# A fused Fourier filter, mixture layer and channel mixer on one core: forward units of batches 1 to 7 spread over more of the tiles

## The chip, the cores and the metric

The kernel runs on one core of a Trainium2 chip. The metric is the time of one execution on the device in microseconds. Before the change it is 3288.33 us, the median of three runs (3287.11 to 3288.41). The engines are named as in the profile: PE (matrix products), PEld (its weight loads), DVE (vector), ACT (scalar), POOL (GpSimd) and SP, which issues nearly all DMAs.

## The reference

Eight sequences of 3072 tokens with 256 channels go through three layers in float32:

```python
X = np.fft.rfft(x, axis=1)
y = np.fft.irfft(X * (filt_r + 1j * filt_i), n=S, axis=1)          # long filter, per channel
h = np.maximum(np.maximum(y @ w1, y @ w2), y @ w3)                 # 256 -> 768
x1 = h @ w_out                                                     # 768 -> 256
prev = x1 shifted by one token within its sequence
xk, xr = mu_k * x1 + (1 - mu_k) * prev, mu_r * x1 + (1 - mu_r) * prev
k = np.maximum(xk @ w_k, 0)                                        # 256 -> 1024
out = 1 / (1 + np.exp(-(xr @ w_r))) * ((k * k) @ w_v)
```

## The kernel before

Every product is made of three: both factors are split into a rounded high part (`xH`, cast by ACT) and the rest (`xL`, subtracted by POOL or DVE), and `mm3` (L121) multiplies high by high, high by low and low by high.

**Three stages.** First batch 0's filter and the weights of the middle layer, to about 150 us. Then the middle layer in 48 tiles of 512 tokens, six to a batch (`t` is the tile, `b` its batch, `g` its place in the batch), and beside tiles 0 to 41 the filter of batches 1 to 7. Last, from about 2060 us, the channel mixer in 48 tiles; the diff does not touch it.

**A tile of the middle layer** has six blocks `fblock` (18 products of 512 columns each; ACT copies the first result, DVE takes the maximum with the other two into `hm`, then `hH` on ACT and `hL` on POOL), then `stage_b` (the last step of the inverse transform of the next tile, products into `y`), then `x1_out` (36 products into `x`). For the next tile `untwiddle` makes `vp` on DVE from `vt`, which `load_v` fetches two tiles ahead from DRAM (`vs`), and ACT and POOL split it (`vH`, `vL`). An ordinary tile has 168 products.

**The filter of a batch** comes from the generator `fft_all` (L321). Its forward part has six units. For each one, `load_x` fetches `xt` (four DMAs, half of them from `xr`, a mirrored copy of x that `mirror_x` writes to DRAM by pairs of batches), `split_x` folds it on POOL (`xe`, two instructions) and splits it (`xH` on ACT, `xL` on POOL, two each), `dft_rows` puts six products into `re` and `im`, and `twiddle` turns these into `A` (per call two scalings `t` on ACT, two DVE instructions). Then for each half `h` of the channels DVE does a 12-point transform (`dft12`), a product with the filter `F`, a 12-point transform back, and the result `T` goes to `vs`. A small side path with four short products treats one frequency apart.

**What sets the order.** Instructions stand on each engine in the order in which the code issues them. `fft_all` yields a cost after each piece, or `STOP`. The `Meter` (L756) is called at 15 steps in a tile, two in each `fblock` and three in `x1_out`. At a step it goes on with the generator until the sum of the costs has reached the share that `share` asks for at this point, and it ends a step at a `STOP`. `done_at` says at which tile each batch's filter is to be done: 5, 11, 17 and so on. A batch costs `FFT_COST`: 6 units of `U_COST` = 2 and 88.6 for the rest, so 100.6, and in six tiles that is 16.8 a tile. `meter.need(b + 1)` at the last tile of a batch finishes that filter; `load_v` of the next tile follows at once there.

The forward units of a batch stand close together: each is `dft_rows`, the load for two units on, the whole split of the next unit, a `STOP`, both twiddles, and a `STOP`. Both halves of the mirroring for a pair are issued ahead of the loads of an odd batch's units.

Of the kernel before, what the change touches and what calls it, by code (L numbers as in the profile page):

```python
# [7 lines left out]
F32 = mybir.dt.float32  # L8
# [5 lines left out]
B, S, D = 8, 3072, 256  # L14
NF = 768
NF2 = 1024
P = 128
NH = D // P
# [74 lines left out]
def tile_fourier_moe_rwkv(ctx, tc, xl, fl, f0, dft24m, dft, idft, tw, w1, w2, w3, wo, muk, mur, wk, wv, wr, out):  # L93
# [162 lines left out]

    def mirror_x(p):
        for h in range(NH):  # L260
            rows = xl[p, h].rearrange("n g ab x -> g ab n x")[:, :, :63:-1]
            if p == 0:
                nc.sync.dma_start(out=xr[p][h].rearrange("(g ab) n x -> g ab n x", ab=2)[:, 1], in_=rows[:, 1])
            else:
                nc.sync.dma_start(out=xr[p][h], in_=rows.rearrange("g ab n x -> (g ab) n x"))

    def fetch_x(xt, b, u):
        lower = xl[b // 2, :, :, u, b % 2].rearrange("h n (o x) -> o n h x", o=2)
        upper = xr[b // 2][:, 2 * u + b % 2].rearrange("h n (o x) -> o n h x", o=2)
        for k in range(2):  # L270
            for odd in range(2):
                if k == 0:
                    rows = lower[odd, :64]
                elif b:
                    rows = upper[1 - odd]
                else:
                    rows = lower[odd, 64:]
                nc.sync.dma_start(out=xt[64 * odd:64 * odd + 64, k].rearrange("p (h x) -> p h x", h=NH), in_=rows)

    def fold(xe, xt, eng):  # L280
        tt(xe[:, 0], xt[:, 0], xt[:, 1], add, eng)
        tt(xe[:, 1], xt[:, 0], xt[:, 1], sub, eng)

    def dft_rows(xH, xL):
        re = bank([P, NH, 2, P], "re")
        im = bank([P, NH, 2, P], "im")
        for k, o in enumerate((re, im)):
            mm3(o.rearrange("p h q c -> p (h q c)"), dftH[:, k], dftL[:, k], xH[:, k], xL[:, k], True, True)
        return re, im
# [30 lines left out]

    def fft_all():  # L321
        xt_t, xs_t, ps_t, f_t = {}, {}, {}, {}

        def load_x(b, u):
            if b < B:
                xt_t[b, u] = fp.tile([P, 2, 512], F32, tag="xt", name="xt", bufs=2)
                fetch_x(xt_t[b, u], b, u)

        def split_x(b, u):
            xt = xt_t.pop((b, u))  # L330
            xe = fp.tile([P, 2, 512], F32, tag="xe", name="xe")
            fold(xe, xt, nc.gpsimd)
            xH = fp.tile([P, 2, 512], F32R, tag="xH", name="xH", bufs=2)
            xL = fp.tile([P, 2, 512], F32R, tag="xL", name="xL", bufs=2)
            for k in range(2):
                nc.scalar.copy(out=xH[:, k], in_=xe[:, k])
                tt(xL[:, k], xe[:, k], f32(xH[:, k]), sub, nc.gpsimd)
            xs_t[b, u] = (xH, xL)

        def twiddle(b, u, A, q):  # L340
            re, im = ps_t[b, u]
            s = 2 * u + q
            t1 = fp.tile([P, NH, P], F32, tag="t1", name="t1", bufs=2)
            t2 = fp.tile([P, NH, P], F32, tag="t2", name="t2", bufs=2)
            scaled(t1, im[:, :, q], nsinv(s))
            scaled(t2, re[:, :, q], sinv(s))
            for r, (a, t) in enumerate(((re, t1), (im, t2))):
                stt(A[:, :, s, r], a[:, :, q], cosv(s), t, mult, add)

        def load_f(h):  # L350
            f_t[h] = fp.tile([P, 2, M2, P], F32, tag="F", name="F")
            nc.sync.dma_start(out=f_t[h], in_=fl[h, :, :, :M2])

        mirror_x(0)
        load_f(0)
        load_x(1, 0)
        load_x(1, 1)
        yield STOP
        yield STOP
        yield STOP  # L360
        split_x(1, 0)
        yield STOP
        yield STOP
        for b in range(1, B):
            A = fp.tile([P, NH, M2, 2, P], F32, tag="A", name="A")
            if b % 2 and b + 1 < B:
                mirror_x((b + 1) // 2)
            for u in range(NU):
                ps_t[b, u] = dft_rows(*xs_t.pop((b, u)))
                if u + 2 < NU:  # L370
                    load_x(b, u + 2)
                if u + 1 < NU:
                    split_x(b, u + 1)
                yield STOP
                for q in range(2):
                    twiddle(b, u, A, q)
                    yield U_COST / 2
                ps_t.pop((b, u))
                yield STOP
            nc.sync.dma_start(out=rs[b].rearrange("(o h) s r c -> o (h s r c)", o=1), in_=A[0:1].rearrange("p h s r c -> p (h s r c)"))  # L380
            sidegen = side(b)
            for h in range(NH):
                X = A[:, h]
                T = fp.tile([P, M2, 2, P], F32, tag="T", name="T", bufs=2)
                F = f_t.pop(h)
                if h == NH - 1:
                    load_x(b + 1, 0)
                    load_x(b + 1, 1)
                fi = F[:, 1].rearrange("p (a s) c -> p a s c", s=4)[:, :, 2:4]
                nc.scalar.mul(out=fi, in_=fi, mul=-1.0)  # L390
                yield from dft12(X, T, 0)
                for g in range(3):
                    sl = slice(4 * g, 4 * g + 4)
                    for r in range(2):
                        tt(X[:, sl, r], T[:, sl, r], F[:, 0, sl], mult)
                    yield 1.3
                    for r in range(2):
                        tt(T[:, sl, r], T[:, sl, r], F[:, 1, sl], mult)
                    yield 1.3
                    tt(X[:, sl, 0], X[:, sl, 0], T[:, sl, 1], sub)  # L400
                    tt(X[:, sl, 1], X[:, sl, 1], T[:, sl, 0], add)
                    yield 1.3
                if b + 1 < B or h + 1 < NH:
                    load_f((h + 1) % NH)
                if h == NH - 1 and b + 1 < B:
                    split_x(b + 1, 0)
                for c in dft12(X, T, 1):
                    yield c
                    if h == NH - 1:
                        next(sidegen, None)  # L410
                nc.sync.dma_start(out=vs[b][:, h], in_=T)
                if h == NH - 1:
                    for _ in sidegen:
                        pass
                    done.add(b)
                yield 0.0
# [175 lines left out]
                    spread_f(c + 1, j)  # L592
            yield

    U_COST = 2.0
    FFT_COST = NU * U_COST + 2 * 44.3


# [284 lines left out]
    with tc.manual_schedule():  # L883
# [49 lines left out]
            pass  # L933


        meter, done_at = Meter(fft_all(), (B - 1) * FFT_COST), [0.0] + [6.0 * b - 1.0 for b in range(1, B)]

        def share(tau):
            for b in range(1, B):
# [5 lines left out]
        for t, (b, g) in enumerate(tiles):  # L945
            if t == len(tiles) - NTILE:
                meter.to(1.0)
                fctx.close()
                p2w = ctx.enter_context(tc.tile_pool(name="p2w", bufs=1, side="right"))
                tctx = ctx.enter_context(ExitStack())  # L950
                p2t = tctx.enter_context(tc.tile_pool(name="p2t", bufs=1, side="right"))
                meter = Meter(load_w2(p2w, p2t), 58.0)
                share = lambda tau, t0=float(t): (tau - t0) / (NTILE - 2)
            at[0] = float(t)

            def step(w):
                at[0] += w / TILE_STEPS
                meter.to(share(at[0]), CAP * w)

            last = t == len(tiles) - 1  # L960
            if last:
                meter.to(1.0)
                tctx.close()
                p2 = ctx.enter_context(tc.tile_pool(name="p2", bufs=1, side="right"))
                load_x1(0, p2)
                load_x1(1, p2)
            edge = g == NTILE - 1
            if edge and not last:
                meter.need(b + 1)
                load_v(t + 1)  # L970
            for f in range(FB1):
                fblock(t, f, step)
                if not last and f in ((2, 4) if edge else (1, 3)):
                    untwiddle(t + 1, f // 2 - 1 if edge else (f - 1) // 2)
                if f == 4 and t + 2 < len(tiles) and g != NTILE - 2:
                    load_v(t + 2)
                if last and f % 2:
                    shift_mix(0, f // 4, (f // 2) % 2, p2)
            y_t.pop(t)
            run_later()  # L980
            if not last:
                stage_b(t + 1)
            x1_out(t, step)
# [98 lines left out]
```

## Time and profile before

| | us |
|---|---|
| median of three runs (range) | 3288.33 (3287.11 to 3288.41) |
| the profiled execution | 3289.4 |
| its span, first to last instruction | 3287.6 |
| PE busy in the span | 3111.7 (95%) |
| DVE, ACT, POOL busy | 2159.7, 1481.7, 1335.0 |
| mean granted clock of PE | 0.978 |

The page gives for each engine the time in which some instruction of it ran. A row of 40 digits cuts the span into 40 slices of 82.2 us. The view by stretches answers the same for any stretch, so a stretch can be laid on a tile: from the first `fblock` product of a tile to the first one of the next. That view rounds to 0.1 us and counts an instruction at a border in both stretches. The waits view names what ended an engine's idle time before an instruction.

### The profile page before, as it was taken

The numbers are of one execution on the slowest core, as the hardware profiler recorded it, in microseconds if no ns is written. First come the engines' busy times: TensorE is split into PE (matmuls) and PEld (weight loads), VectorE is DVE, ScalarE is ACT, GpSimd is POOL, SyncE is SP. The second block draws the span as 40 slices with busy tenths as digits, with TensorE's granted clock in tenths as the row PEclk, the third lists the DMA queues.
The fourth block names the chain that finished last, engine by engine and source line by source line (L and its number), as shares of the span: only waits on it lengthen the run. The fifth ranks groups of instructions, "written<-read, shape, count | busy, mean of one in ns | idle before, by whom it ended". The sixth has DMA issues, their size and how long they took to land. (4 is left out here: it accounts for less than half of the span.)

```text
span 3287.6 us, 43694 instructions
## 1 busy us (share of the span) xinstructions
PE 3111.7 (95%) x16596; PEld 2644.5 (80%) x16596; DVE 2159.7 (66%) x2825; ACT 1481.7 (45%) x2744; POOL 1335.0 (41%) x988
## 2 busy tenths in 40 slices
PE   4689899799999899899999999999999999999999
PEld 2368688688788688788788888888999899989998
DVE  3769688588688588688587553555555565556555
ACT  3643333333433433433433443555555555555554
POOL 2263633533534523534533333344434443444433
PEclk7999999899999999999999999999999999999999
DMA  5622212312212312221211210111111111111110
GB/s 147 190 92 77 91 46 60 127 46 70 79 46 84 103 45 84 65 90 39 78 65 40 77 52 32 52 52 58 49 52 52 58 49 49 52 57 53 49 52 33
DMA packets 110743, 221.37 MB, mean 67 GB/s; under 512 B 11477, under 2 KB 51773, under 8 KB 108733
## 3 DMA queue, kind: packets, MB, share of 16 engines
q1 hardware_dynamic: 106244, 213.86, 20.1%
q10 hardware_dynamic: 4288, 4.72, 0.6%
q8 instruction: 130, 2.13, 0.3%
q14 instruction: 81, 0.66, 0.1%
HBM read 139.55 MB, written 90.00 MB: 70 GB/s over the span
## 5 line engine op out<-in xcount | busy, mean ns | idle before, releaser
L127 POOL TENSOR_TENSOR hL<-hm,hH 128x512 fp32r<-128x512 f32 x288 | 416.7, 1447 | 942.0 <-ACT hH L730 928.7
L127 DVE TENSOR_TENSOR hm<-p,hm 128x512 f32<-128x512 f32 x576 | 394.4, 686 | 325.9 <-PE p L124 260.6
L124 PE MATMUL pv<-wvh,kl 128*128 128x256 f32 x1536 | 433.0, 282 | 9.7 <-POOL kl L127 8.3
L127 POOL TENSOR_TENSOR ml<-tm,mh 128x512 fp32r<-128x512 f32 x192 | 248.6, 1295 | 456.3 <-ACT mh L819 456.3
L123 PE MATMUL pv<-wvl,kh 128*128 128x256 f32 x1536 | 428.1, 279 | 0.0
L122 PE MATMUL pv<-wvh,kh 128*128 128x256 f32 x1536 | 428.0, 279 | 0.0
L127 POOL TENSOR_TENSOR kl<-sq,kh 128x512 fp32r<-128x512 f32 x192 | 248.3, 1293 | 267.8 <-ACT kh L843 106.9
L722 ACT COPY hm<-p 128x512 f32<-128x512 f32 x288 | 168.6, 586 | 396.7 <-PE p L124 396.5
L819 ACT CAST mh<-tm 128x512 fp32r<-128x512 f32 x192 | 119.1, 620 | 495.4 <-DVE tm L130 495.4
L124 PEld LDWEIGHTS pv<-wvh,kl 128*128 128x128 f32 x1536 | 289.7, 189 | 19.5 <-POOL kl L127 19.5
L123 PE MATMUL pk<-ml,wkh 128*128 128x512 f32 x768 | 303.3, 395 | 0.1
L122 PE MATMUL pk<-mh,wkh 128*128 128x512 f32 x768 | 300.2, 391 | 0.0
L124 PE MATMUL pk<-mh,wkl 128*128 128x512 f32 x768 | 299.7, 390 | 0.0
L122 PEld LDWEIGHTS pv<-wvh,kh 128*128 128x128 f32 x1536 | 290.2, 189 | 0.0
L123 PEld LDWEIGHTS pv<-wvl,kh 128*128 128x128 f32 x1536 | 288.4, 188 | 0.0
L130 DVE SCALAR_TENSOR_TENSOR sq<-pk,rl 128x512 f32<-128x512 f32 x384 | 249.7, 680 | 58.2 <-ACT rl L838 58.2
L130 DVE SCALAR_TENSOR_TENSOR tm<-xt,mu_sb,tm 128x512 f32<-128x512 f32 x192 | 194.3, 1012 | 131.5 <-ACT tm L139 131.5
L730 ACT CAST hH<-hm 128x512 fp32r<-128x512 f32 x288 | 179.4, 623 | 189.6 <-DVE hm L127 189.0
L127 DVE TENSOR_TENSOR ot<-pv,sg 128x512 f32<-128x512 f32 x96 | 66.4, 692 | 301.4 <-issue 223.8
L127 DVE TENSOR_TENSOR kl<-sq,kh 128x512 fp32r<-128x512 f32 x192 | 221.3, 1152 | 31.7 <-ACT kh L843 15.6
L843 ACT ACTIVATE kh<-rl 128x512 fp32r<-128x512 f32 x384 | 240.8, 641 | 0.0
L122 PE MATMUL p<-yH,w1h 128*128 128x512 f32 x576 | 229.3, 398 | 2.6 <-DVE hm L127 1.9
(163 smaller groups left out, 8140.5 us busy)
## 6 DMA issues: line engine op xcount, KB each, us to landing
xt<-x1s SPq DMA_DIRECT2D x40, 768.0 KB
x1s<-xo SPq DMA_DIRECT2D x96, 256.0 KB
out_dram<-ot SPq DMA_DIRECT2D x96, 256.0 KB
F<-in_fl_dram SPq DMA_DIRECT2D x14, 1536.0 KB
vs<-T SPq DMA_DIRECT2D x14, 1536.0 KB
vt<-vs SPq DMA_DIRECT2D x42, 512.0 KB
xt<-in_xl_dram SPq DMA_DIRECT2D x108, 128.0 KB
xt<-xr SPq DMA_DIRECT2D x84, 128.0 KB
```

Of the source, the lines that this page charges most:

```text
L122: nc.tensor.matmul(o, lh, rh, start=first, stop=False)
L123: nc.tensor.matmul(o, lh, rl, start=False, stop=False)
L124: nc.tensor.matmul(o, ll, rh, start=False, stop=last)
L127: (eng or nc.vector).tensor_tensor(out=o, in0=a, in1=b, op=op)
L130: nc.vector.scalar_tensor_tensor(out=o, in0=a, scalar=s, in1=b, op0=op0, op1=op1)
L722: nc.scalar.copy(out=hm, in_=ps[0])
L730: nc.scalar.copy(out=hH, in_=hm)
L819: nc.scalar.copy(out=hi, in_=tf)
L843: nc.scalar.activation(out=kh, in_=rl, func=AF.Square)
```

## The change

The diff spreads the units. `split_x` becomes a generator of three pieces (fold; first half of the split; second half), and these stand between the two twiddles of the unit before. Units are counted through all batches, x is fetched two units ahead also across the end of a batch, and so the first unit of a batch is split before the transforms of the batch before it. `U_COST` goes from 2 to 6, so a batch costs 124.6. Each half of a mirroring stands apart: for batches 2 and 3 behind the loads in the first two units of batch 1, later ones ahead of the two halves of an even batch's transforms. From batch 2 on, `done_at` is 10.3, 16.3, 22.3 and so on; `meter.need` and the load of the next batch's first tile move into the last tile but one, behind its fifth `fblock`. Batch 1's filter still has to be done at tile 5, and its load stays there.

```diff
-        def split_x(b, u):
-            xt = xt_t.pop((b, u))
+        units = [(b, u) for b in range(1, B) for u in range(NU)]
...
+        def split_x(i):
+            if i == len(units):
+                return
+            xt = xt_t.pop(i)
             xe = fp.tile([P, 2, 512], F32, tag="xe", name="xe")
             fold(xe, xt, nc.gpsimd)
+            yield
...
             for k in range(2):
                 nc.scalar.copy(out=xH[:, k], in_=xe[:, k])
                 tt(xL[:, k], xe[:, k], f32(xH[:, k]), sub, nc.gpsimd)
+                if k == 0:
+                    yield
...
             for u in range(NU):
-                ps_t[b, u] = dft_rows(*xs_t.pop((b, u)))
-                if u + 2 < NU:
-                    load_x(b, u + 2)
-                if u + 1 < NU:
-                    split_x(b, u + 1)
+                i = NU * (b - 1) + u
+                ps_t[u] = dft_rows(*xs_t.pop(i))
+                load_x(i + 2)
+                if b == 1 and u < NH:
+                    mirror_x(1, u)
                 yield STOP
-                for q in range(2):
-                    twiddle(b, u, A, q)
-                    yield U_COST / 2
-                ps_t.pop((b, u))
-                yield STOP
+                sgen = split_x(i + 1)
+                twiddle(b, u, A, 0)
+                yield U_COST / 6
+                next(sgen, None)
+                yield U_COST / 4
+                twiddle(b, u, A, 1)
+                ps_t.pop(u)
+                yield U_COST / 6
+                next(sgen, None)
+                yield 5 * U_COST / 24
+                next(sgen, None)
+                yield 5 * U_COST / 24
...
-                if h == NH - 1:
-                    load_x(b + 1, 0)
-                    load_x(b + 1, 1)
+                if b in (2, 4):
+                    mirror_x(b // 2 + 1, h)
...
-    U_COST = 2.0
+    U_COST = 6.0
...
-        meter, done_at = Meter(fft_all(), (B - 1) * FFT_COST), [0.0] + [6.0 * b - 1.0 for b in range(1, B)]
+        meter, done_at = Meter(fft_all(), (B - 1) * FFT_COST), [0.0] + [6.0 * b - (1.7 if b > 1 else 1.0) for b in range(1, B)]
...
-            edge = g == NTILE - 1
-            if edge and not last:
+            edge = t == NTILE - 1
+            if edge:
                 meter.need(b + 1)
                 load_v(t + 1)
...
-                if f == 4 and t + 2 < len(tiles) and g != NTILE - 2:
+                if f == 4 and t + 2 < len(tiles) and t != NTILE - 2:
+                    if g == NTILE - 2:
+                        meter.need(b + 1)
                     load_v(t + 2)
```

On POOL, around tiles 10 and 11 (the end of batch 1, where the units of batch 3 run): `xe` and `xL` belong to units, `hL` to blocks, `vL` to the next tile. Before:

```order
L127 TENSOR_TENSOR xe_4758<-xt_3955 128x512 x2
L127 TENSOR_TENSOR xL_4762<-xe_4758,xH_4761 128x512 x2
L127 TENSOR_TENSOR xe_4837<-xt_4753 128x512 x2
L127 TENSOR_TENSOR xL_4841<-xe_4837,xH_4840 128x512 x2
L127 TENSOR_TENSOR hL_4821<-hm_4819,hH_4820 128x512
L127 TENSOR_TENSOR xe_4900<-xt_4832 128x512 x2
L127 TENSOR_TENSOR xL_4904<-xe_4900,xH_4903 128x512 x2
L127 TENSOR_TENSOR hL_4882<-hm_4880,hH_4881 128x512
```

After:

```order
L127 TENSOR_TENSOR xe_4940<-xt_4823 128x512 x2
L127 TENSOR_TENSOR hL_4929<-hm_4927,hH_4928 128x512
L127 TENSOR_TENSOR vL_4958<-vp_4952,vH_4957 128x512
L127 TENSOR_TENSOR xL_4990<-xe_4940,xH_4989 128x512 x2
L127 TENSOR_TENSOR hL_4982<-hm_4980,hH_4981 128x512
L127 TENSOR_TENSOR xe_5044<-xt_4901 128x512 x2
L127 TENSOR_TENSOR hL_5019<-hm_5017,hH_5018 128x512
L127 TENSOR_TENSOR vL_5055<-vp_5049,vH_5054 128x512
```

Before, one block's `hL` stands between two whole units; now the fold and the split of a unit are apart, with blocks between them.

On DVE, in tile 13 (the second of batch 2, beside transforms of batch 3): `hm` belongs to blocks, `T` and `A` to the transforms and the product with `F`. Before, its first two blocks:

```order
L127 TENSOR_TENSOR hm_5549<-p1_5529,hm_5549 128x512
L127 TENSOR_TENSOR hm_5549<-p2_5530,hm_5549 128x512
L127 TENSOR_TENSOR T_5194<-T_5194,F_4440 128x4x128 x2
L127 TENSOR_TENSOR hm_5578<-p1_5558,hm_5578 128x512
L127 TENSOR_TENSOR hm_5578<-p2_5559,hm_5578 128x512
L127 TENSOR_TENSOR A_4742<-A_4742,T_5194 128x4x128 x2
```

After:

```order
L127 TENSOR_TENSOR hm_5564<-p1_5544,hm_5564 128x512
L127 TENSOR_TENSOR A_4546<-A_4546,T_5237 128x4x128 x2
L127 TENSOR_TENSOR hm_5564<-p2_5545,hm_5564 128x512
L127 TENSOR_TENSOR A_4546<-T_5237,F_4348 128x4x128 x2
L127 TENSOR_TENSOR hm_5595<-p1_5575,hm_5595 128x512
L127 TENSOR_TENSOR T_5237<-T_5237,F_4348 128x4x128 x2
L127 TENSOR_TENSOR hm_5595<-p2_5576,hm_5595 128x512
L127 TENSOR_TENSOR A_4546<-A_4546,T_5237 128x4x128 x2
```

Behind the same four maxima eight instructions of the filter now stand where four stood, some of them between the two maxima of a block.

On SP, at the start of batch 3's units: `xr` is the mirroring, `xt` a unit's x. Before:

```order
L319 DMA vs2_60<-svo_4640 24x128 x2
L265 DMA xr2_75<-in_xl_dram 768x1x512 x2
L278 DMA xt_4753<-in_xl_dram 64x2x256 x2
L278 DMA xt_4753<-xr1_74 64x2x256 x2
L751 DMA x1s1_78<-xo_4791 128x512 x2
L669 DMA vt_4796<-vs2_60 128x2x512
```

After:

```order
L318 DMA vs2_60<-svo_4473 24x128 x2
L277 DMA xt_4555<-in_xl_dram 64x2x256 x2
L277 DMA xt_4555<-xr1_74 64x2x256 x2
L277 DMA xt_4698<-in_xl_dram 64x2x256 x2
L277 DMA xt_4698<-xr1_74 64x2x256 x2
L678 DMA vt_4703<-vs2_60 128x2x512
```

The two mirrorings no longer stand there, two units are fetched first, and `vt` of the next batch's first tile follows in the last tile but one.

## Rows read from the trace of the kernel before

**Rows 1.** The page: PE in 40 slices, and its granted clock.
```profile
PE   4689899799999899899999999999999999999999
PEclk7999999899999999999999999999999999999999
```

**Rows 2.** Stretches laid on tiles: length, busy (instructions) by engine, PE clock, DMA.
```profile
151.30:210.00 58.70, 48.17 (x200) 36.69 (x200) 33.66 (x56) 33.67 (x65) 44.49 (x35) 0.94 0.50 165
210.00:257.10 47.10, 39.86 (x176) 32.11 (x175) 41.29 (x54) 14.61 (x29) 12.11 (x8) 0.96 0.07 23
257.10:292.60 35.50, 35.50 (x170) 29.87 (x169) 34.87 (x41) 12.56 (x24) 12.47 (x8) 1.00 0.31 97
...
328.10:368.30 40.20, 38.37 (x181) 31.43 (x180) 36.31 (x42) 15.09 (x29) 25.88 (x16) 1.00 0.15 54
368.30:429.60 61.30, 50.82 (x199) 39.09 (x198) 30.30 (x52) 25.67 (x54) 31.27 (x25) 0.89 0.28 87
...
465.20:500.70 35.50, 35.50 (x170) 29.88 (x169) 30.36 (x38) 11.81 (x23) 12.75 (x8) 1.00 0.21 75
...
571.80:610.10 38.30, 38.30 (x181) 31.43 (x180) 36.87 (x41) 14.60 (x29) 21.15 (x13) 1.00 0.20 67
610.10:677.00 66.90, 48.26 (x200) 37.23 (x199) 26.12 (x44) 25.58 (x54) 30.47 (x24) 0.87 0.37 121
...
857.50:917.60 60.10, 51.18 (x199) 39.45 (x198) 29.70 (x49) 25.21 (x53) 32.85 (x24) 0.89 0.23 63
...
1059.80:1099.50 39.70, 39.70 (x187) 32.55 (x186) 28.13 (x39) 14.61 (x29) 19.18 (x13) 1.00 0.21 81
1099.50:1161.30 61.80, 46.81 (x194) 36.84 (x193) 30.66 (x48) 25.21 (x52) 32.37 (x24) 0.86 0.30 94
...
1343.20:1396.90 53.70, 45.09 (x193) 35.61 (x192) 34.73 (x49) 25.16 (x52) 31.43 (x24) 0.94 0.20 54
...
1579.90:1632.40 52.50, 45.96 (x193) 37.03 (x192) 34.39 (x50) 23.11 (x48) 26.22 (x21) 0.90 0.19 51
...
1811.50:1847.00 35.50, 35.50 (x169) 29.92 (x168) 11.26 (x18) 11.70 (x23) 10.27 (x8) 1.00 0.14 45
1847.00:1887.00 40.00, 37.77 (x170) 31.22 (x170) 30.44 (x44) 22.20 (x39) 16.12 (x11) 0.96 0.32 106
```

**Rows 3.** Timeline of POOL in tile 11: start, length, instruction, idle time before.
```profile
631.91 2.48 POOL L127 TENSOR_TENSOR xe<-xt 128x512 f32<-128x512 f32 x2 [23.90 <-DMA xt<-xr]
634.35 2.50 POOL L127 TENSOR_TENSOR xL<-xe,xH 128x512 fp32r<-128x512 f32 x2
...
639.88 2.51 POOL L127 TENSOR_TENSOR xe<-xt 128x512 f32<-128x512 f32 x2
642.35 2.54 POOL L127 TENSOR_TENSOR xL<-xe,xH 128x512 fp32r<-128x512 f32 x2
...
647.95 2.53 POOL L127 TENSOR_TENSOR xe<-xt 128x512 f32<-128x512 f32 x2
```

**Rows 4.** Waits of PE in tile 11: total us, times, longest.
```profile
PE re L122 <- ACT xH L336: 14.0, 1, 14.0
PE re L123 <- POOL xL L127: 3.6, 3, 1.3
```

**Rows 5.** Waits of PE in tile 29.
```profile
PE y L122 <- ACT vH L688: 5.7, 1, 5.7
```

**Rows 6.** Waits of PE from 150 to 175 us, in tile 0.
```profile
PE re L122 <- ACT xH L336: 4.4, 1, 4.4
```

**Rows 7.** Timeline of DVE in tiles 11 and 12.
```profile
643.81 0.48 DVE L130 SCALAR_TENSOR_TENSOR A<-re,tw_sb,t 128x256 f32<-128x256 f32 x1 [3.95 <-ACT t L139]
...
664.05 0.87 DVE L130 SCALAR_TENSOR_TENSOR vp<-vt,tw_sb,b 128x256 f32<-128x256 f32 x2
...
687.87 1.91 DVE L130 SCALAR_TENSOR_TENSOR vp<-vt,tw_sb,b 128x256 f32<-128x256 f32 x2
```

**Rows 8.** Timeline of POOL in tile 12, the `hL` beside the last of those.
```profile
687.92 1.58 POOL L127 TENSOR_TENSOR hL<-hm,hH 128x512 fp32r<-128x512 f32 x1 [2.78 <-ACT hH L730]
```

More of the change, by code (lines that the diff above doesn't have):

```diff
@@ L255, in tile_fourier_moe_rwkv, with mirror_x @@
     NU = NTILE
[L259 to L265, printed above, removed]
+    def mirror_x(p, h):
+        rows = xl[p, h].rearrange("n g ab x -> g ab n x")[:, :, :63:-1]
+        if p == 0:
+            nc.sync.dma_start(out=xr[p][h].rearrange("(g ab) n x -> g ab n x", ab=2)[:, 1], in_=rows[:, 1])
+        else:
+            nc.sync.dma_start(out=xr[p][h], in_=rows.rearrange("g ab n x -> (g ab) n x"))
     def fetch_x(xt, b, u):
@@ L322, in fft_all, with load_x @@
         xt_t, xs_t, ps_t, f_t = {}, {}, {}, {}
[L324 to L327, printed above, removed]
-        def split_x(b, u):
-            xt = xt_t.pop((b, u))
+        units = [(b, u) for b in range(1, B) for u in range(NU)]
+        def load_x(i):
+            if i < len(units):
+                xt_t[i] = fp.tile([P, 2, 512], F32, tag="xt", name="xt", bufs=2)
+                fetch_x(xt_t[i], *units[i])
+        def split_x(i):
+            if i == len(units):
+                return
+            xt = xt_t.pop(i)
             xe = fp.tile([P, 2, 512], F32, tag="xe", name="xe")
             fold(xe, xt, nc.gpsimd)
+            yield
             xH = fp.tile([P, 2, 512], F32R, tag="xH", name="xH", bufs=2)
@@ L337, in split_x @@
                 tt(xL[:, k], xe[:, k], f32(xH[:, k]), sub, nc.gpsimd)
-            xs_t[b, u] = (xH, xL)
+                if k == 0:
+                    yield
+            xs_t[i] = (xH, xL)
         def twiddle(b, u, A, q):
-            re, im = ps_t[b, u]
+            re, im = ps_t[u]
             s = 2 * u + q
@@ L352, in load_f @@
             nc.sync.dma_start(out=f_t[h], in_=fl[h, :, :, :M2])
-        mirror_x(0)
+        for h in range(NH):
+            mirror_x(0, h)
         load_f(0)
-        load_x(1, 0)
-        load_x(1, 1)
+        load_x(0)
+        load_x(1)
         yield STOP
@@ L360, in fft_all @@
         yield STOP
-        split_x(1, 0)
+        for _ in split_x(0):
+            pass
         yield STOP
@@ L365, in fft_all @@
             A = fp.tile([P, NH, M2, 2, P], F32, tag="A", name="A")
-            if b % 2 and b + 1 < B:
-                mirror_x((b + 1) // 2)
             for u in range(NU):
-                ps_t[b, u] = dft_rows(*xs_t.pop((b, u)))
-                if u + 2 < NU:
-                    load_x(b, u + 2)
-                if u + 1 < NU:
-                    split_x(b, u + 1)
-                yield STOP
-                for q in range(2):
-                    twiddle(b, u, A, q)
-                    yield U_COST / 2
-                ps_t.pop((b, u))
-                yield STOP
+                i = NU * (b - 1) + u
[3 more added lines that the diff above has]
+                    mirror_x(1, u)
+                yield STOP
+                sgen = split_x(i + 1)
[10 more added lines that the diff above has]
+                yield 5 * U_COST / 24
             nc.sync.dma_start(out=rs[b].rearrange("(o h) s r c -> o (h s r c)", o=1), in_=A[0:1].rearrange("p h s r c -> p (h s r c)"))
@@ L404, in fft_all @@
                     load_f((h + 1) % NH)
-                if h == NH - 1 and b + 1 < B:
-                    split_x(b + 1, 0)
                 for c in dft12(X, T, 1):
```

## The prediction

> **What bounds the kernel now.** The page first: PE is at 9 tenths or more nearly everywhere, with dips to 8 and one to 4 in the first half, and its granted clock dips at the same places [rows 1]. So the second half, untouched by the diff, is bound by PE, and the question is what the dips are. The view by stretches, laid on tiles, answers it [rows 2]. An ordinary tile takes 35.5 us with PE busy all the time at clock 1.00, as from 465.2. Instructions above 168 (one or two belong to the border) tell the units in a tile, six products each. The tile from 1059.8 has two units and the side path, the one from 571.8 one unit and the side path: 39.7 - 38.3 = 1.4 us a unit, and 38.3 - 35.5 - 1.4 = 1.4 for the side path. Neither loses anything. The last tile of each batch does. What each tile takes beyond 35.5 and its units is lost:
>
> tile 0 (five units) 58.7 - 42.5 = 16.2; tile 1 (one) 47.1 - 36.9 = 10.2; tile 4 (one, side path) 40.2 - 38.3 = 1.9; tiles 5, 11 and 17 (five each) 18.8, 24.4 and 17.6; tiles 23, 29 and 35 (four each, against 41.1) 20.7, 12.6 and 11.4; tile 42, from 1847, 4.5. The sum is 138.3 us; all other tiles run at PE's pace.
>
> Why tiles with units lose is seen on POOL: a fold takes 2.5 us and a split 2.5, and folds start 8.1 us apart (639.88, 647.95), with a block's `hL` between [rows 3]. PE has a block's 18 products (18 x 1.4 / 6 = 4.2 us) and a unit's 1.4 in that time, 5.6 us of work. ACT casts `xH` in order ahead of the next `hm` copy, so it passes POOL's delay on. In tile 11, 23.9 us of it is POOL waiting for x behind both mirrorings [rows 3], of which PE sees 14.0 [rows 4]. The clock then falls to means of 0.86 to 0.94 in these tiles [rows 2], which costs PE again. In tiles 29 and 35 most is another wait: 5.7 us for the `vH` of the next batch's first tile in tile 29 [rows 5], whose load is issued only when the last tile begins.
>
> **The change, part by part.** No product, no vector instruction and no DMA is added or dropped; the same ones stand elsewhere.
>
> *Units spread.* At 20.8 cost a tile, a unit of 6 takes 0.29 tile, 10.3 us. POOL needs 5.0 for it [rows 3] and 0.29 of the 10.27 that a tile's eight `hL` and `vL` take (tile from 1811.5) [rows 2], 3.0: 8.0 of 10.3, where before it was asked for more than it had. The fold is issued a quarter of a unit ahead of the cast that needs it, so ACT no longer waits in front of `hm`. What is left is a wait of PE for the last `xL`, issued shortly ahead of `dft_rows`. Its bounds are nothing and the 1.2 us that each such wait takes now [rows 4], 0 to 43 us for 36 units outside batch 1; I take 1 us a batch, 6 us, near the lower end, because POOL now has time to spare and PE has a part of a block queued ahead of the product.
>
> *x two units ahead, mirrorings moved.* The 14.0 us in tile 11 goes, and with it the like in tile 23. Each half mirroring now stands on SP ahead of one `vt` load; both halves and the loads behind them cost POOL 23.9 us, so one half is under 12, and `vt` is wanted 0.68 tile (24 us) after its issue. I cost it at nothing; if the cover went, four waits of up to 12 us, 48, are the other end.
>
> *The load of the next batch's first tile* comes 0.47 tile (17 us) earlier, so the wait of [rows 5] and its like go, except at tile 5, whose path is the old one: 4 us stay there (0 to 6).
>
> *Transforms compressed.* This is the price. Without the filter DVE is busy 11.3 us a tile (from 1811.5), with transforms at 16.8 cost a tile 30.4 (from 465.2), so they take 19.1 [rows 2]. At 20.8 they take 19.1 x 1.238 = 23.7, and DVE 35.0 of 35.5. That this still hides is shown by the tile from 257.1: DVE is at 34.87 and PE loses nothing [rows 2]. So batches 3 to 7 get 2 us in all. Batch 2 has 5.3 tiles in place of six, 23.5 a tile: 26.8 + 11.3 = 38.1, 2.6 over in some 3.8 tiles, 10 us; PE's banks and light blocks let DVE lag by a few, so 5 (0 to 10). Batch 1 has five tiles, 24.9 a tile: 28.4 + 11.3 = 39.7, 4.2 over in some 3.5 tiles, 15 us, of which I take 10 (3 to 18).
>
> How much of those 19.1 us is DVE standing still beside POOL decides the ratio. Two `vp` instructions take 0.87 us at 664.05 and 1.91 at 687.87 [rows 7], where an `hL` of POOL runs for 1.58 [rows 8]: 1.04 lost. Eight such a tile are 8.3 us. If all eight already hit, the work grows only by (19.1 - 8.3) x 0.238 = 2.6, and DVE needs 33.0; if none hit and all would, 23.7 + 8.3 + 11.3 = 43.3. The ratio's 35.0 lies near the lower end, and I keep it. The Trainium skill says in "SBUF — State Buffer", section "Who interferes with whom", that a vector instruction with two SBUF inputs and a GpSimd instruction that reads SBUF exclude each other for the whole instruction, and that one with a single SBUF input does not contend. By that rule a denser DVE meets more of POOL's instructions, which speaks against this change; the trace agrees on the exclusion (1.91 against 0.87), and also that a `twiddle` from PSUM keeps its 0.48 us at 643.81 [rows 7] while POOL splits from 642.35 [rows 3].
>
> *Batch 1's start.* The first unit's x arrives as late as before: 4.4 us of PE's wait for its `xH` [rows 6] stay, with the cold clock behind it. The rest of tile 0's 16.2 is the POOL chain, now with half a mirroring between x loads: 10 stay (6 to 16). Tile 1's 10.2 came with a DVE at 41.3 [rows 2], the first transforms having begun; now the last units are there, and the transforms come later: 2 (0 to 6). Tile 42's 4.5 stays: it is the load of the last weights.
>
> **Sum.** Lost after: 10 + 2 + 10 + 4 + 5 + 2 + 6 + 4.5 = 43.5 us against 138.3, a gain of 94.8. The profiled execution took 3289.4, so 3194.6; it stands 1.1 above the median, so 3194 (rounded).
>
> **Rivals.**
> First: *DVE becomes the bound.* If a denser DVE meets nearly every `hL` and `vL`, a transform tile needs the middle of 33.0 and 43.3, 38. For it: the exclusion above. Against it: the tile from 257.1, where 34.87 hides. Price: 2.5 x 4.3 tiles x 5 batches = 53 in place of 2, and 10 more in batches 1 and 2: lost 105, so 3255. The skill's rule by itself gives this case.
> Second: *units still wait for POOL*, 1.2 us each as now [rows 4]: 43 in place of 6, so 3231. For it: `xL` is issued close ahead of its product; against it: POOL's 8.0 of 10.3 us.
> Third, the other side: *DVE bound, and far.* Some 3.5 + 3.8 + 5 x 4.3 = 28.8 tiles carry transforms. The other losses sum to 26.5; the gain is gone when each such tile is (138.3 - 26.5) / 28.8 = 3.9 over, that is from a DVE need of 39.4 us. At 40.5, 5.0 over, the time is 3289.4 - 138.3 + 26.5 + 144 = 3322. Against it: it needs most of what the upper bound allows.
> Fourth: *the change does not do what it says*, the units bunch up again since each ends a step at its `STOP` and the meter catches up behind it: about 3289. A step is 1/15 of a tile on average and a unit takes four, so this is unlikely.
>
> **How the numbers follow.** Forecast 0.74, first rival 0.12, second 0.08, third 0.04, fourth 0.02. The forecast's own range is 3166 (lost 15: tile 0's lower bound 6, 3 in batch 1, 4.5 in tile 42, little else) to 3222 (lost 71: the upper ends of tiles 0, 1 and 5 and of batches 1 and 2, 5 in later batches, units and tile 42 as taken). The range that leaves out no more than 2 in 10 takes in the second rival: 3166 to 3240. Less than 0.2% (6.6 us) is about what a measurement of this kernel can't tell from no change: faster 0.94, the same 0.02, slower 0.04.
>
> **What would show it.** In the stretches, tiles 11, 17, 23, 29 and 35 fall to 35.5 plus 1.4 a unit and the clock stays at 1.00; folds on POOL stand about 10 us apart; no wait for `xt` behind `xr`. Transform tiles of batches 3 to 7 stay at 35.5 with DVE at 34 to 35.5; tiles 2 to 4 and 7 to 9 are longer. If transform tiles are 37 or more throughout, with PE waiting for `hm`, the first or third rival holds; if PE waits for `xL` at each unit, the second.

## The result and the profile after

The changed kernel takes 3208.19 us, the median of four runs (3206.90 to 3208.91), against 3287.72 (3286.60 to 3288.41) for the kernel before, measured beside it: a ratio of 0.9759, 95% interval 0.9747 to 0.9771. It is 79.5 us faster; 3194 was predicted, in a range of 3166 to 3240. The profiled execution took 3208.55, its span 3206.8, the mean granted clock rose from 0.978 to 0.986.

The page after, PE in 40 slices and its granted clock, against [rows 1]:

```profile
PE   4689999999999999999999999999999999999999
PEclk7989999999999999999999999999999999999999
```

The dips behind the third slice are gone. Stretches laid on tiles 0, 1, 3, 4, 5, 8, 9, 11, 14, 16, 17 and 34, columns as in [rows 2]:

```profile
149.70:213.90 64.20, 51.56 (x200) 39.22 (x200) 31.28 (x54) 31.96 (x61) 40.27 (x32) 0.87 0.49 160
213.90:251.80 37.90, 37.30 (x176) 30.98 (x175) 28.35 (x36) 16.99 (x34) 22.71 (x16) 1.00 0.14 43
...
288.30:327.40 39.10, 37.59 (x169) 31.38 (x168) 38.68 (x47) 12.53 (x24) 13.16 (x8) 0.96 0.22 68
327.40:369.80 42.40, 40.08 (x182) 32.61 (x181) 41.57 (x51) 12.81 (x25) 17.58 (x10) 0.96 0.14 51
369.80:417.00 47.20, 42.31 (x194) 34.08 (x193) 22.70 (x40) 21.89 (x46) 28.80 (x23) 1.00 0.40 124
...
489.50:529.10 39.60, 37.51 (x169) 31.35 (x168) 38.52 (x44) 12.67 (x24) 12.40 (x8) 0.96 0.28 107
529.10:569.90 40.80, 38.64 (x175) 31.39 (x173) 40.35 (x54) 11.49 (x22) 12.80 (x8) 0.96 0.18 65
...
609.90:650.10 40.20, 39.98 (x187) 33.16 (x186) 19.91 (x33) 21.64 (x45) 29.36 (x22) 1.00 0.22 67
...
721.20:756.70 35.50, 35.50 (x169) 29.89 (x168) 33.71 (x40) 12.67 (x24) 12.70 (x8) 1.00 0.21 74
793.90:835.60 41.70, 41.53 (x194) 34.36 (x193) 21.29 (x37) 20.21 (x42) 26.09 (x21) 1.00 0.34 114
835.60:875.60 40.00, 38.61 (x182) 32.04 (x180) 20.02 (x32) 19.53 (x40) 26.11 (x20) 1.00 0.21 63
...
1471.20:1516.40 45.20, 41.90 (x187) 34.32 (x186) 20.56 (x33) 19.89 (x42) 25.77 (x20) 0.96 0.32 106
```

Read as in the prediction, 35.5 a tile, 1.4 a unit and 1.4 for the side path are no loss. Tile 11 falls from 66.9 us with five units to 40.2 with three, tile 17 from 60.1 with five to 40.0 with two, both at clock 1.00. Tile 14, full of transforms, takes 35.5 with DVE at 33.7. But tile 0 rises from 58.7 to 64.2 at a clock of 0.87, and tiles 8 and 9, batch 2's compressed transforms, lose 4.1 and 3.9.

POOL's timeline, columns as in [rows 3], has folds 9.6 and 11.1 us apart here. From the second to the last unit of a batch, the mean step is 10.7 to 12.5 us in batches 2 to 7, single steps go from 6.4 to 18.5, and no fold there waits for x:

```profile
619.36 2.55 POOL L127 TENSOR_TENSOR xe<-xt 128x512 f32<-128x512 f32 x2
...
628.91 2.55 POOL L127 TENSOR_TENSOR xe<-xt 128x512 f32<-128x512 f32 x2
...
640.05 2.54 POOL L127 TENSOR_TENSOR xe<-xt 128x512 f32<-128x512 f32 x2
```

PE's waits from 216 to 1860 us (total, times, longest); before, from 216 to 2062 us, `re` waited 28.3 us for `xH` and `y` 17.3 for `vH`:

```profile
PE im L123 <- POOL xL L127: 9.8, 12, 1.5
PE y L124 <- POOL vL L127: 5.3, 6, 2.3
PE sx L302 <- DMA side_in<-rs: 3.8, 2, 2.1
PE re L123 <- POOL xL L127: 2.2, 1, 2.2
PE y L122 <- ACT vH L697: 1.9, 3, 1.2
PE im L122 <- ACT xH L339: 1.8, 1, 1.8
```

From the first product of tile 0 to the first of tile 47 it is 1801.6 us, before 1877.8: 76.2 gained, where the prediction had 94.8. The other 4.6 of the span's 80.8 lie outside (1405.2 against 1409.8), in code that the diff leaves alone.

### The profile page after: what moved, and what is told of

Its sections match the earlier page's. It is cut to its first block, busy times and chain, and to the rows that moved or that the text cites. A ratio compares the mean times of both kernels' runs of the same rounds, so it can differ in the third digit from the quotient of the medians.

```text
span 3206.8 us, 43665 instructions
## 1 busy us (share of the span) xinstructions
PE 3085.1 (96%) x16596; PEld 2629.2 (82%) x16596; DVE 2142.3 (67%) x2825; ACT 1474.6 (46%) x2744; POOL 1340.1 (42%) x988
## 5 line engine op out<-in xcount | busy, mean ns | idle before, releaser
L127 POOL TENSOR_TENSOR hL<-hm,hH 128x512 fp32r<-128x512 f32 x288 | 435.2, 1511 | 864.3 <-ACT hH L739 862.5
L847 ACT ACTIVATE rl<-pk 128x512 f32<-128x512 f32 x384 | 226.8, 603 | 4.4 <-DMA x1s<-xo 2.3
```

The source lines that it names most:

```text
L127: (eng or nc.vector).tensor_tensor(out=o, in0=a, in1=b, op=op)
L847: nc.scalar.activation(out=rl, in_=ps, func=AF.Relu)
```

## The experiments

Each ratio is against the kernel before on the same chip, with its 95% interval; that kernel's median was between 3287.6 and 3291.5 on the chips used, so times from different chips differ by some us for that alone. "Tiles" is the stretch of 47 tiles in the trace, as just defined; it comes from one execution, which for "late" was the fastest of four (3198.78) and for "late, whole" the slowest (3208.39). "Whole" is a split issued in one piece ahead of the twiddles, as before the change; "pieces" is the changed order; "early" and "late" are the request in the last tile but one and at the last tile's start.

| kernel | median us | ratio (interval) | tiles us |
|---|---|---|---|
| before | 3287.72 | 1 | 1877.8 |
| x ahead | 3291.86 | 1.0014 (1.0005 to 1.0023) | 1880.0 |
| cost 2, pieces | 3334.78 | 1.0130 (1.0115 to 1.0146) | 1921.3 |
| cost 2, whole | 3251.23 | 0.9881 (0.9866 to 0.9895) | 1838.4 |
| changed kernel | 3208.19 | 0.9759 (0.9747 to 0.9771) | 1801.6 |
| mirrorings back | 3217.20 | 0.9774 (0.9758 to 0.9790) | 1805.3 |
| cost 9 | 3260.64 | 0.9906 (0.9890 to 0.9923) | 1851.2 |
| late | 3204.46 | 0.9733 (0.9718 to 0.9747) | 1786.9 |
| batch 1 whole | 3207.03 | 0.9745 (0.9730 to 0.9759) | 1793.8 |
| whole | 3196.50 | 0.9714 (0.9700 to 0.9729) | 1784.2 |
| late, batch 1 whole | 3192.87 | 0.9703 (0.9689 to 0.9718) | 1780.9 |
| late, whole | 3200.86 | 0.9741 (0.9728 to 0.9754) | 1792.5 |
| late, whole but batch 2 | 3200.67 | 0.9738 (0.9724 to 0.9751) | 1788.1 |
| late, whole, cost 5 | 3215.65 | 0.9780 (0.9767 to 0.9794) | 1804.4 |

### The spread undone

```diff
-    U_COST = 6.0
+    U_COST = 2.0
```

> The changed kernel with a unit's cost back at 2 in place of 6, so that four or more units fall into one tile again; mirrorings, early loads and the early request stay as changed. Theory A (the spread itself gives most of the gain): tiles 5, 11, 17, 23, 29 and 35 lose 6 to 12 us each again through POOL's chain, with folds some 8 us apart and a clock below 1.00 there, transforms get lighter by a few us: 3245 to 3280. Rival B (the gain is the removed waits for x and vH, the spread adds nothing): 3203 to 3215.

It took 3334.78: the direction was theory A's, the size was in neither. Five units in tile 5 take 71.6 us, where five took 61.3 before. ACT's timeline in tile 22, columns as in [rows 3], shows the reason:

```profile
1100.90 0.48 ACT L139 ACTIVATE t<-im,tw_sb 128x256 f32<-128x256 f32 x1 [3.12 <-PE im L124]
...
1102.69 0.48 ACT L139 ACTIVATE t<-im,tw_sb 128x256 f32<-128x256 f32 x1 [0.95 <-DVE A L130]
...
1103.42 0.62 ACT L339 CAST xH<-xe 128x512 fp32r<-128x512 f32 x1
```

When the meter catches up, the pieces run together, and the next unit's `xH` stands on ACT behind this unit's twiddles, which wait for this unit's `im`. So each unit's products start a chain PE, ACT, DVE, ACT, POOL that ends at the next unit's products. To part this from the crowding, the order was put back too:

```diff
-                yield STOP
                 sgen = split_x(i + 1)
+                for _ in sgen:
+                    pass
+                yield STOP
...
+    U_COST = 2.0
```

> The changed kernel with a unit's cost back at 2 and each unit's whole split issued behind its products and ahead of its twiddles, both as before the change; what stays changed is x fetched two units ahead, the places of the mirrorings and the early request. Theory A (crowding alone costs what the prediction put on POOL's chain; the run with cost 2 and the new order of pieces rose to 3335 because there the pieces stand behind the twiddles): tiles 5, 10, 16, 22, 28 and 34 lose 8 to 15 us each, the time 3240 to 3265. Rival B (the new order was the whole damage, crowding costs little once x is there in time): 3200 to 3220. Rival C (crowding costs the same in either order): 3320 to 3340.

3251.23, theory A. With crowded units the new order alone costs 1921.3 - 1838.4 = 82.9 us of tiles. With the whole split the spread is worth 3251.23 - 3196.50 = 54.7 (the run at cost 6 is below).

One part of the change runs through all these kernels: the diff also drops the `STOP` that ended each unit. When the meter is behind, a unit takes one step where it took two, so at cost 2 the units are more crowded than before. In the run at cost 2 with the whole split, tile 0 holds six units (five before), and the five folds from 586.4 to 613.8 us start 6.9 us apart on average, against 8.0 in [rows 3]. The 54.7 us are the price of that crowding; no run puts the `STOP` back, so what it is worth alone is not shown.

### The mirrorings and x two ahead

```diff
+            if b % 2 and b + 1 < B:
+                for h in range(NH):
+                    mirror_x((b + 1) // 2, h)
...
-                if b == 1 and u < NH:
-                    mirror_x(1, u)
...
-                if b in (2, 4):
-                    mirror_x(b // 2 + 1, h)
```

> The changed kernel with both halves of a mirroring issued together ahead of the first unit of batches 1, 3 and 5, as before the change; x still fetched two units ahead, all else as changed. Theory A (the place of the mirrorings matters): the loads of units 2 and 3 of batches 3 and 5 stand behind 23.9 us of mirroring while units come 10 us apart, PE waits 4 to 14 us in each, and some in batch 1: 3216 to 3240. Rival B (x two units ahead hides it alone): 3204 to 3213.

The median, 3217.20, lies in theory A's range, on a chip where the kernel before took 3291.51; the traces side with rival B. The tiles differ by 3.7 us in all, 1.8 of it in tile 42, the intervals overlap, and the waits of 4 to 14 us that theory A names are not there: the longest for x's halves is 2.2. With units some 10 us apart, x two units ahead covers both mirrorings but for one fold's 3.94 us on POOL. The other way round, x ahead on the kernel before (units at 2, whole split, late request, mirrorings together, but still without the `STOP` behind each unit):

```diff
-                if u + 2 < NU:
-                    load_x(b, u + 2)
-                if u + 1 < NU:
-                    split_x(b, u + 1)
+                load_x(i + 2)
+                for _ in split_x(i + 1):
+                    pass
...
-                if h == NH - 1:
-                    load_x(b + 1, 0)
-                    load_x(b + 1, 1)
```

> The kernel before with one part alone: x fetched two units ahead across the batches, and with it each batch's first split behind the last unit of the batch before. Units cost 2, mirrorings both ahead of the odd batches, the whole split ahead of the twiddles, the late request. Theory A (x two units ahead is worth what the run with cost 2 and the whole split showed, 39 us, whatever the mirrorings' place): 3245 to 3262. Rival B (with units crowded, the third and fourth load stand behind both mirrorings and the wait of 14 us comes back): 3262 to 3285.

Both ranges missed: it gains nothing (1.0014). POOL's timeline in tile 11:

```profile
625.71 2.48 POOL L127 TENSOR_TENSOR xe<-xt 128x512 f32<-128x512 f32 x2 [22.46 <-DMA xt<-xr]
```

The wait of [rows 3], 23.9 us, is back with 22.46, and PE waits 15.8 us there for `xH` (14.0 in [rows 4]). That is rival B's mechanism. So, as far as these runs go, fetching ahead pays only where the units are spread or the mirrorings stand elsewhere; a price of the dropped `STOP` may hide in this. With crowded units the mirrorings' place (and the early request, changed along with it) is worth 1880.0 - 1838.4 = 41.6 us of tiles.

### The early request

```diff
-            edge = t == NTILE - 1
-            if edge:
+            edge = g == NTILE - 1
+            if edge and not last:
...
-                if f == 4 and t + 2 < len(tiles) and t != NTILE - 2:
-                    if g == NTILE - 2:
-                        meter.need(b + 1)
+                if f == 4 and t + 2 < len(tiles) and g != NTILE - 2:
...
-(1.7 if b > 1 else 1.0)
+1.0
```

> The changed kernel with transforms due at the end of the last tile again (six tiles a batch) and the next batch's first tile loaded when the last tile begins; spread and mirrorings as changed. Theory A (this is a third part of the gain): the wait for vH, 5.7 us in tile 29 before, comes back at batches 2 to 6, 3 to 6 us each, five times, against some 4 us won back where transforms are less dense: 3219 to 3234. Rival B (that wait was a by-product of the crowded POOL and goes with the spread): 3202 to 3211.

Rival B, and better than the changed kernel: by 14.7 us of tiles, but in the fastest of its four executions, and 3.1 of it in tile 0, whose order the edit leaves alone. The ratios, 0.9733 and 0.9759, are some 8.5 us apart, and their intervals touch. PE's wait for `vH` over 216 to 1860 us, then tiles 8 and 9:

```profile
PE y L122 <- ACT vH L697: 0.6, 1, 0.6
```

```profile
488.80:524.30 35.50, 35.50 (x169) 29.88 (x168) 35.12 (x43) 12.67 (x24) 13.68 (x8) 1.00 0.23 86
524.40:559.90 35.50, 35.50 (x170) 29.87 (x168) 34.08 (x45) 11.81 (x23) 12.65 (x8) 1.00 0.30 105
```

The waits of [rows 5] do not come back with the old request, so the load was not their cause. The trace of the kernel before shows what was, on DVE and ACT in tile 29:

```profile
1378.57 4.49 DVE L127 TENSOR_TENSOR T<-A 128x1536 f32<-128x1536 f32 x2
1382.98 0.87 DVE L130 SCALAR_TENSOR_TENSOR vp<-vt,tw_sb,b 128x256 f32<-128x256 f32 x2
...
1383.88 0.62 ACT L688 CAST vH<-vp 128x512 fp32r<-128x512 f32 x1 [4.22 <-DVE vp L130]
```

Nothing there waits for the load. `vp` stands on DVE behind the first transforms of the next batch, 4.49 us of them; with cheap units these began in the batch's last tile (eleven of their instructions in tile 29). With units at 6 the units reach through the whole last tile, and in this run it has none of them. What the early request did was to compress batch 2, and without it tiles 8 and 9 lose nothing; DVE hides at 35.12.

### Batch 1's order, and the whole split

```diff
-                yield STOP
                 sgen = split_x(i + 1)
+                if b == 1:
+                    for _ in sgen:
+                        pass
+                yield STOP
```

> The changed kernel in which, for batch 1 alone, a unit's whole split (fold, casts, differences) is issued right behind the unit's products and ahead of its twiddles, as before the change. Theory A (tile 0 lost 21.6 us against 16.1 before because the pieces run together there and now stand behind the twiddles, so the next unit's xH waits for this unit's im): tile 0 falls from 64.2 to 56 to 59 us, the time to 3196 to 3204. Rival B (half a mirroring between x loads, or the cold start, makes it): tile 0 stays at 62 or more, 3206 to 3210.

Tile 0 does what theory A says, 55.3 us (12.8 lost in place of 21.7), and the tiles gain 7.8; the median is 3 above the range, in rival B's, on a chip where the kernel before took 3291.51, and its interval overlaps the changed kernel's, so the reading rests on tile 0. ACT in tile 0, first of the changed kernel, then of this one:

```profile
186.80 0.47 ACT L139 ACTIVATE t<-im,tw_sb 128x256 f32<-128x256 f32 x1 [1.00 <-DVE A L130]
...
187.53 0.62 ACT L339 CAST xH<-xe 128x512 fp32r<-128x512 f32 x1
```

```profile
182.96 0.62 ACT L339 CAST xH<-xe 128x512 fp32r<-128x512 f32 x1 [0.84 <-POOL xe L127]
...
184.75 0.47 ACT L139 ACTIVATE t<-im,tw_sb 128x256 f32<-128x256 f32 x1
```

In the one, the cast stands behind the twiddles' `t`; in the other ahead of them. PE's waits in tile 0, without the longest, the first unit's for `xH`, come to 8.1 us in the changed kernel and 3.8 here; the granted clock over the tile is 0.87 there and 0.94 here. Then the same for all batches:

```diff
-                yield STOP
                 sgen = split_x(i + 1)
+                for _ in sgen:
+                    pass
+                yield STOP
```

> The changed kernel, a unit's cost at 6, with the whole split of the next unit issued behind a unit's products and ahead of its twiddles, in all batches, as before the change. Theory A (the split must be cut in pieces, or ACT's casts stand in front of the next copy of hm while POOL folds): PE loses 1 to 2 us at each of 36 units, 3228 to 3270. Rival B (with units 10 us apart POOL has time in either order, and the last xL comes earlier than now): waits for xL go, tile 0 falls to 55 to 56 us, 3190 to 3202.

Rival B: 3196.50, tile 0 at 55.1. Over 216 to 1860 us PE's waits are no longer for `im`'s `xL` but for `vH` and `hm`:

```profile
PE y L124 <- POOL vL L127: 6.1, 6, 2.3
PE y L122 <- ACT vH L699: 5.5, 4, 3.1
PE p L122 <- ACT hm L733: 3.1, 1, 3.1
```

Tile 5 takes 52.7 us in place of 47.2 and carries the last of these; tiles 8 and 9 still lose.

### The gains together

The diffs of the late request and of batch 1's whole split, both:

> The late request (transforms due at the end of the last tile, run before at 3204) together with batch 1's split ahead of its twiddles (which took tile 0 from 64.2 to 55.3 us). Theory A (the two are independent: lighter transforms in six tiles, and no serial chain in tile 0): 3194 to 3201, and tiles 0 to 1 at 55 and 37 us. Rival B (batch 1's earlier end is eaten by its transforms, which are due later anyway): 3202 to 3208.

Theory A, 1 us below its range: 0.9703 against the changed kernel's 0.9759, intervals apart. By its median this is the fastest kernel of the study; the whole split alone, 3196.50 on the same chip, has an interval that overlaps, though all four of its executions took longer. With the late request's diff and that of the whole split in all batches:

> The two edits that gained, together: the request at the last tile's start with transforms due at its end (3204 alone), and every unit's split issued whole ahead of its twiddles (3197 alone). Theory A (they are independent: the first saves tiles 8 and 9, the second tile 0 and the waits for the last xL): the 7.5 us of waits for im's xL go, 3180 to 3190, which beats both kernels. Rival B (tile 5, which rose from 47.2 to 52.7 us with the whole split, rises here too): 3190 to 3198.

Both theories missed, 3200.86. The two edits are not independent: the wait for `vH`, 0.5 us in the run before, is 12.2 in six places, and tile 11 takes 47.6 us against 42.2. ACT in tile 11, of this kernel, then of the one before it:

```profile
608.12 0.62 ACT L339 CAST xH<-xe 128x512 fp32r<-128x512 f32 x1 [6.72 <-POOL xe L127]
...
620.47 0.62 ACT L339 CAST xH<-xe 128x512 fp32r<-128x512 f32 x1 [3.19 <-POOL xe L127]
...
625.88 0.62 ACT L699 CAST vH<-vp 128x512 fp32r<-128x512 f32 x1 [1.74 <-DVE vp L130]
```

```profile
612.14 1.14 ACT L339 CAST xH<-xe 128x512 fp32r<-128x512 f32 x2
...
620.65 0.62 ACT L700 CAST vH<-vp 128x512 fp32r<-128x512 f32 x1
```

With the whole split ACT stands in front of the fold (6.72 and 3.19 us), and the untwiddling of the next batch's first tile, which the late request puts into the same tile, stands behind it. The first fold itself waits 4.03 us for x. In pieces the fold has run by the time ACT comes to the cast. So pieces and early request cover one wait (1.9 us with both, 0.5 with the pieces alone, 5.5 with the early request alone, 12.2 with neither), each at a price: the pieces at the waits for `xL`, the request at batch 2's transforms.

```diff
-                for _ in sgen:
-                    pass
+                if b != 2:
+                    for _ in sgen:
+                        pass
```

> As the run before, but batch 2 keeps the split in pieces, since tile 5, where batch 2's units begin beside batch 1's last transforms, lost 5.5 us more with the whole split. Theory A (there the whole split puts ACT's casts in front of hm and vH): tile 5 stays at 47 us, 2 to 6 us below the run with the whole split in all batches, 3178 to 3188. Rival B (tile 5's loss in that run came from the early request): no difference above 2 us, 3180 to 3192.

The difference is rival B's, the absolute time missed as in the run before: tile 5 is at 47.6 against 48.7. It took 47.2 with the early request and pieces, so its 52.7 needed the early request and the whole split together.

```diff
-    U_COST = 6.0
+    U_COST = 5.0
```

> The late request and the whole split, with a unit's cost at 5 in place of 6: transforms a twentieth lighter (19.8 cost a tile), units 9.0 us apart against POOL's need of 5.0 + 2.6. Theory A (batch 1 and 2, whose transforms still fill DVE, gain 2 to 6 us, the units lose nothing): 2 to 6 us below the same kernel at cost 6. Rival B (POOL's chain becomes short at 9.0 us): 2 to 10 us above it.

Rival B, beyond its range: 14.8 us above. Tile 23 takes 50.2 in place of 41.2 and tile 35 49.0 in place of 43.2. In tile 23 PE waits 4.2 us for `vH` and its granted clock is 0.93, against no wait and 1.00 at cost 6. Folds come 9 to 12 us apart there, at cost 6 they came 6 to 12 apart, so a lack of time on POOL, rival B's reason, is not shown. The wait is for the same instruction as in tile 11 above; why cost 5 lengthens it stays open.

### The price of dense transforms

```diff
-    U_COST = 6.0
+    U_COST = 9.0
```

> The changed kernel with a unit's cost at 9 in place of 6: transforms of batches 3 to 7 run at 23.8 cost a tile in place of 20.8. Theory A (DVE is nearly full at 20.8 and its work grows in proportion): a transform tile needs 19.1 x 23.8 / 16.8 + 11.3 = 38.4 us, 2.9 over 35.5 in some 3.5 tiles of five batches, 50, and 20 to 30 more in batches 1 and 2: 3265 to 3295. Rival B (some of DVE's time is collision with POOL that does not grow with density): 3 to 4 us less in each such tile, transform tiles of batches 3 to 7 stay near 35.5, 3210 to 3235. Rival C (units further apart also end the waits for xL): below 3208.

Nearest theory A, 4 us under its range. Tiles 13 to 15:

```profile
706.50:742.60 36.10, 35.75 (x169) 29.93 (x169) 33.63 (x43) 11.83 (x23) 11.97 (x8) 1.00 0.22 71
742.70:783.10 40.40, 37.48 (x170) 31.34 (x169) 39.71 (x46) 12.49 (x24) 12.12 (x8) 0.96 0.19 67
783.10:824.70 41.60, 39.09 (x176) 31.73 (x175) 40.87 (x54) 12.23 (x24) 13.68 (x8) 0.96 0.18 65
```

DVE is busy 98% of tiles 14 and 15, and PE waits. At 23.8 cost a tile the tiles 12 to 41 lose 41 us, where scaling gave 50; 33 of it in tiles without units, which lost under 1 at 20.8. The step from hidden to bound lies between. Single tiles do not follow the scaling: tiles 14 and 15 needed 40 us, tile 13 only 36, where it gave 38.4 for each. The stretch from tile 12 to tile 42, for the kernel before, the changed one and this one:

```profile
677.00:1847.00 1170.00, 1130.15 (x5215) 936.63 (x5214) 878.80 (x1143) 430.10 (x819) 490.04 (x336) 0.98 0.21 67
650.10:1770.10 1120.00, 1111.50 (x5216) 926.84 (x5215) 871.86 (x1145) 424.58 (x817) 488.33 (x332) 1.00 0.20 69
669.60:1818.70 1149.10, 1122.85 (x5221) 936.29 (x5220) 867.84 (x1150) 426.95 (x825) 482.63 (x337) 0.99 0.20 68
```

For nearly the same instructions DVE is busy 878.8, 871.9 and 867.8 us. Packed into fewer tiles they take neither longer, as the prediction's first rival had it, nor much less, as rival B here had it; what binds is the same work in fewer tiles.

## Why the prediction was right, and where not

The mechanism was right, the size 18.6 us too good inside the tiles (76.2 against 94.8); 4.6 us outside, which no term foresaw, hid part of that by luck. By its steps, lost after:

- **Tile 0: 10 predicted (6 to 16), 21.7 measured.** This is the step that failed: "the rest of tile 0's 16.2 is the POOL chain, now with half a mirroring between x loads". It took the pieces to be apart everywhere. In batch 1 the meter is behind from the start, the pieces run together, and their new order puts `xH` behind the twiddles; POOL was not the chain: it was busy 40.3 of the tile's 64.2 us, before 44.5 of 58.7. With the old order in batch 1, 12.8 are lost. The half mirroring stayed.
- **Units of batches 2 to 7: 6 predicted (0 to 43), about 13 measured**, in tiles 10 to 35. The term was near the lower end and rightly so, but mis-sized: `im` waits for the last `xL` 12 times, 9.8 us, and tile 34 loses 5.5 with its clock at 0.96. With the whole split these waits go, so the new order makes them; the second rival, 43, did not come.
- **x and the mirrorings: 0 predicted.** Behind tile 0 no fold waits for x, and the run with the mirrorings back shows that the fetch ahead covers them by itself, but for one fold, once the units are spread.
- **The early request: the waits of [rows 5] go.** They went, but the reason was wrong: the wait was for DVE, where the next batch's transforms stood ahead of `vp`, and without the early request it goes as well. Its own price, batch 2's tiles at 5 (0 to 10), measured 8.0 in tiles 8 and 9.
- **Batch 1's end:** tile 1 at 2, measured 1.0; tiles 2 to 4 at 10, measured 8.7; tile 5 at 4 (0 to 6), measured 6.1, just outside, and not by the wait named there: PE waits 4.9 us for `xL` in that tile and not for `vH`.
- **Batches 3 to 7, transforms: 2 predicted, under 1 measured**, DVE at 32.5 and 33.7 in tiles 13 and 14, where 35.0 was worked out. The first and third rivals needed 38 and 39.4; neither came. DVE still stands beside POOL, as in [rows 7]; its timeline in tile 14:

```profile
733.32 1.90 DVE L130 SCALAR_TENSOR_TENSOR vp<-vt,tw_sb,b 128x256 f32<-128x256 f32 x2
```

An `hL` of POOL runs for 2.09 us from 732.45. But the time lost to it in all did not grow with the density, as DVE's 878.8, 871.9 and 867.8 us above show. The Trainium skill says in "SBUF — State Buffer", section "Who interferes with whom", that two such instructions exclude each other. The trace agrees: 1.90 here against 0.87 in [rows 7]. The rival that a denser DVE meets nearly all of POOL's instructions and is the bound at 20.8 did not come.

- **Tiles 42 and 43: 4.5 predicted, 3.6 measured.**
- **That it would not do what it says** (fourth rival, units bunch up): not in batches 2 to 7, where folds stand 11 to 12 us apart on average; in batch 1 the catching up it named is what made tile 0 worse.

## What to carry to other kernels

Where work is cut into pieces between steps that a meter gives out, work out the order that results when the meter is behind and all pieces run in one step: in-order engines then see the pieces behind their neighbours, and a chain across engines may close. Spreading the work over more tiles removed two waits for which remedies had been added as well; try each remedy without the others, since one of them (the early request) then only costs. Before a wait is put down to a load, look at what stands ahead of it on the engine that it waits for. Look also for what a rewrite drops on the way, as the `STOP` here. Here DVE, busy for 35.12 of a tile's 35.5 us, still hid; beyond that, what it needed more came out as time.

## What the runs showed that was not expected

The order of the pieces costs 82.9 us of tiles with crowded units and 17.4 with spread ones (1801.6 against 1784.2): the parts of the change depend on each other, and with the spread left out the rest of it makes the kernel 1.3% slower. Outside the 47 tiles the same code takes 1405.2 us in the changed kernel's profile, 1409 to 1411 in most others and 1414 to 1416 in three of the last four runs; what makes this isn't settled, and it is as large as the last gains compared here, so these were read from the tiles.
